# Soft mixture of experts behind attention: fp32 output product on four row groups, and where the expert weights are put

## The chip, the core and the metric

The kernel runs on one core of one Trainium2 chip. A core has TensorE (PE; its weight loads are shown apart as PEld), VectorE (DVE), ScalarE (ACT), GpSimd (POOL) and SyncE (SP); here SP issues all DMAs, in the order of its own program, and 16 DMA engines move the data. The metric is the device time of one execution in microseconds, the median of several runs.

## The reference

Causal attention with a decay bias, over 8 batches, 8 heads, 576 tokens and 64 features a head; its output, 4608 tokens by 512, goes through a soft mixture of 8 experts with 4 slots each.

```python
scores = q @ k.T / sqrt(64);  bias = min(-(cum[t] - cum[s]), 0)   # cum: running sum of max(s, 0)
attn = softmax(where(causal, scores + bias, -1e9));  x = attn @ v   # x: [4608, 512]
logits = x @ phi                                                    # [4608, 32]
d = softmax over tokens (logits);  slot_input = d.T @ x             # [32, 512], 4 slots an expert
h = max(slot_input[e] @ w1[e], 0);  slot_out[e] = h @ w2[e]         # w1 [512, 1024], w2 [1024, 512]
c = softmax over slots (logits);  out = c @ slot_out                # [4608, 512] in fp32
```

The expert weights are 32 MB, the output is 9.4 MB; all of it is fp32 in memory.

## The kernel before, in words

**Attention.** 64 heads are worked off as 32 pairs (p = 0 to 31), four pairs a batch. For each pair: load, cast into a high and a low part, row maxima, scores, exponentials, causal cuts, product with v, normalisation, and transposes back to rows of tokens. At the end of each batch the logits are formed (`lt`, L632 and L636) and the slot inputs are summed up (`t2` to `t8`). `e_nat` keeps the 32 exponentials of each token, divided by their sum (`s2p`, on POOL), as five chunks a batch: four of 128 tokens and one of 64.

**Order.** Every step is an entry of `ops` with an engine, a cost, a due time and what it comes after. `schedule` (L44) makes the order from these, for all engines; the steps of the last stretch are left out of it and follow in an order written out by hand in `END` (L33). Each engine works strictly in its own order. SP's loads and fetches are entries like the others.

**Weights.** Each expert matrix is cut into 4 quarters of 512 KB, [128, 1024] in SBUF; w1 and w2 together have 64. `seq` (L897) lists them in the order of use: all of w1, then w2 for the first half of the output columns, then w2 for the second. `pre` is a buffer for 21 quarters (`NPRE`) that are loaded during attention. 22 more (`room`, L883, steps `get`) go to places that attention is done with: three slots `g`, one slot `w` of two places, and 17 places of the `arena`, a buffer that holds attention's working tiles side by side. `ended` (L876) says after which steps a tile of the arena is dead. That makes 43; the other 21 are loaded (`refill`, L963) over w1 quarters that the first expert product has used.

**Experts.** `mlp1` (L970) multiplies the 32 slot inputs (`sit`) with w1 for four experts at a time, on four groups of 32 columns; `relu` and `turn` (L988) give the transposed hidden values. `mlp2` (L1000) does the second product for one half of the output columns and four experts, in 8 steps of 4 groups. `pick` (L1011) takes each slot's row of its own expert with two 0/1 matrices, `sel`, that are part of the constants loaded early (`cst_sb`).

**Output.** For each batch `sp` splits `e_nat` into a rounded part, a rest, and the rounded part again (3 x 32 columns), `ct` (L719) transposes the five chunks on TensorE, and `cd` copies them to SBUF: 96 rows of slots by tokens. These stand between the steps of the second product's first half (loop at L1070). `pick` leaves the picked rows in three parts too, split in the same way. The output product (L1038) is then one pass in fp32r with 96 rows, 128 tokens by 256 columns each; two go into one PSUM bank, VectorE and ScalarE copy the banks out in turn (L1040, L1042), and every 8 tiles or 512 KB a DMA writes 512 tokens' half rows (L1046). `result(0)` runs beside the second product's second half, `result(1)` after it.

Of the kernel before, what the change touches and what calls it, by code (L numbers as in the profile page):

```python
# [30 lines left out]
NPRE = 21  # L31

END = """  # L33
s.31.0 ev.29 load_v.31 z.30.3 s.31.3 rd.29 ex.31.0.0 s.31.1 ex.31.0.1 rd.28 cut.31.0 s.31.2 ex.31.1.1 ex.31.1.0
sm.30 ex.31.3.1 get.4 ex.31.3.0 a.30.0 ex.31.2.0 e1.7.1.0 cut.31.3 ex.31.2.1 a.30.1 zc.31 cut.31.2 cut.31.1
z.31.0 a.30.2 a.30.3 nr.29 a.30.4 rb.30 ev.30 get.8 z.31.1 get.9 get.7 a.31.0 z.31.2 z.31.3 ax.31 a.31.1 nr.28
evx.31 nr.30 sm.31 a.31.2 e1.7.2.0 get.14 a.31.3 a.31.4 rb.31 ev.31 get.13 get.12 t5.6 nr.31 lt.28 t6.6 lt.29
get.16 lt.30 get.10 lt.31 t7.6 get.15 c0.7 t2.7 nat0.7 t8.6 t3.7 nat.30 nat.28 natd.30 m.0 nat.29 natd0.7 t4.7
nat.31 m.1 natd.28 get.18 t5.7 natd.29 get.11 natd.31 m.2 get.17 t6.7 m.3 m.4 busy.3 t7.7 m.5 c1.7 t8.7 get.21
m.6 get.19 m.7 get.20 s0.7 busy.5 sit.0 s1.7 sit.1 s2.7 s2p.7 s2p.6  # L40
# [72 lines left out]
def tile_attn_softmoe(ctx: ExitStack, tc, qk, v, s, phi, w1, w2, cst, out):  # L113
# [17 lines left out]
    cst_sb = top.tile([128, 2 * 96 + 128], F32, name="cst_sb")  # L131
    sel = [cst_sb[:, 0:96], cst_sb[:, 96:192]]
    g4 = cst_sb[:, 192:320]
# [13 lines left out]
    sit = top.tile([128, DM // 128, NS], F32, name="sit")  # L147
# [6 lines left out]
    size = dict(raw=2 * S, p=3200, u=S, v=640, z=2 * S, r=S, x=NCH * DM)  # L154
    place = [(kind, (NP + i) % n) for kind, n in (("raw", NR), ("p", NPB), ("z", NZ), ("v", NV), ("r", NQ), ("u", NU), ("x", 1))
             for i in range(n)]
    ar, o = {}, 0
    for key in place:
        ar[key] = o
        o += size[key[0]]  # L160
    arena = top.tile([128, o], F32, name="arena")
# [36 lines left out]
    onesl = one.tile([128, 4 * HP, 32], F32, name="onesl")  # L198
    nc.vector.memset(onesl, 0.0)
    for a in range(4 * HP):  # L200
        nc.vector.memset(onesl[:, a, a:a + 1], 1.0)
# [8 lines left out]
    ph = one.tile([128, HP, 4 * NS], F32, name="ph")  # L210
# [10 lines left out]
    for i, t in enumerate(gs):  # L221
        if i == 1:

            mask = one.tile([128, S], F32, name="mask")
            nc.gpsimd.memset(mask, 0.0)
            nc.gpsimd.affine_select(mask[:, S - 128:S], mask[:, S - 128:S], pattern=[[-1, 128]], compare_op=ALU.is_ge,
                                    fill=NEG, base=0, channel_multiplier=1)
# [36 lines left out]
    def scores(p):  # L264
# [59 lines left out]
        def red(i, a):  # L324
# [125 lines left out]
    def pair(p):  # L450
# [55 lines left out]
        def sm():  # L506
# [93 lines left out]
    late_ct = []  # L600

    def batch(b):
# [21 lines left out]
        def lt(hp):  # L624
# [6 lines left out]
            for g in range(4):  # L631
                nc.tensor.matmul(st["lt", b][32 * g:32 * g + 32, 64:192], ph[:, hp, 32 * g:32 * g + 32],  # L632
                                 st["u", p][:, 64 + 128 * g:192 + 128 * g], start=hp == 0, stop=hp == HP - 1)

            for g in range(4):
                nc.tensor.matmul(st["lt", b][32 * g:32 * g + 32, 0:64], ph[:, hp, 32 * g:32 * g + 32],  # L636
# [22 lines left out]
        def c0():  # L659
            l = p2.tile([128, 192], F32, tag="ls", name=f"ls{b}", bufs=1)  # L660
# [45 lines left out]

        def sp(i):
            x = e_nat[:, b * NCH:(b + 1) * NCH, :]
            if i == 0:
                st["en", b] = p2.tile([128, NCH, 3, NS], F32R, tag="en", name=f"en{b}")  # L710
            en = st["en", b]
            if i == 0:
                nc.vector.tensor_copy(en[:, :, 0, :], x)
            elif i == 1:
                nc.scalar.copy(en[:, :, 2, :], x)
            else:
                nc.vector.tensor_tensor(en[:, :, 1, :], x, en[:, :, 0, :].bitcast(F32), op=ALU.subtract)

        def ct():  # L719
            en = st.pop(("en", b))  # L720
            st["ct", b] = pa, pb = bank(f"cta{b}"), bank(f"ctb{b}")
            for c in range(NCH):
                dst = pa[0:96, 128 * (c - 1):128 * c] if c else pb[0:96, 0:128]
                nc.tensor.transpose(dst, en[:, (c - 1) % NCH].rearrange("p l s -> p (l s)").bitcast(F32), ident)  # L724

        def cd():
            if "ctw" not in st:
                st["ctw"] = [slot("w", [96, min(4, B - 4 * i), S], F32R, f"ct{i}") for i in range((B + 3) // 4)]
            ct = st["ctw"][b // 4][:, b % 4]
            pa, pb = st.pop(("ct", b))  # L730
            copy = nc.vector.tensor_copy if b % 2 else nc.scalar.copy
            copy(ct[:, 64:576], pa[0:96, :])
            copy(ct[:, 0:64], pb[0:96, 0:64])
        late_ct.append((sp, ct, cd))
# [69 lines left out]
    def m1():  # L804
        mrow = one.tile([1, 4, NS], F32, name="mrow")
# [39 lines left out]
    def sit1():  # L845
        nc.vector.tensor_copy(sit, st.pop("sit")[:, 0:128].rearrange("p (c s) -> p c s", c=NCC))
# [23 lines left out]
    op(("cst",), "SP", 450, (3.0,), (fetch, cst_sb, cst), [("load", 3)], dma=450)  # L870
    op(("cw",), "SP", 450, (2.5,), lambda: nc.sync.dma_start(out=cumd, in_=cumhl), [("cum", 1)], dma=800)
    op(("phi",), "SP", 650, (2.0,), load_phi, [("load", 2)], dma=728)
# [3 lines left out]
    def ended(kind, i):  # L876
        n = dict(raw=NR, p=NPB, z=NZ, v=NV, r=NQ, u=NU, x=1)[kind]
# [3 lines left out]
                    x=[("t7", B - 1)])[kind]  # L881
# [7 lines left out]
    for i in range(o // F):  # L889
# [80 lines left out]
    def mlp1(eg):  # L970
        pss = [bank(f"m1{eg}{half}") for half in range(F // 512)]
        for cc in range(NCC):
            for half in range(F // 512):
                for g in range(4):
                    nc.tensor.matmul(pss[half][32 * g:32 * g + 32, :], sit[:, cc, :],
# [22 lines left out]
    sl = []  # L998
# [12 lines left out]
    def pick(half):  # L1011

        ps = bank(f"sel{half}")
        for eg in range(2):
            nc.tensor.matmul(ps[0:96, 0:HC], sel[eg], sos[half][:, eg, :], start=(eg == 0), stop=(eg == 1))  # L1015
        t = sl[half]
        nc.scalar.copy(t, ps[0:96, 0:HC])  # L1017
        nc.vector.tensor_tensor(t[64:96, :], ps[64:96, 0:HC], t[64:96, :].bitcast(F32), op=ALU.subtract)  # L1018

    NO = NT // 128  # L1020
# [5 lines left out]
    def result(half, beside=iter(()), pace=()):  # L1026
        k = 0
        outc = out[:, HC * half:HC * half + HC].rearrange("(t p) c -> p t c", p=128)
        for i in range(0, NO, 4):
            m = min(4, NO - i)  # L1030
            ot = stage.pop(0)[:, 0:m * HC].rearrange("p (t c) -> p t c", t=m)
            for j in range(0, m, 2):
                n = min(2, m - j)
                po = bank(f"po{half}_{i + j}")[:, 0:n * HC].rearrange("p (t c) -> p t c", t=n)
                for x in range(n):
                    b, c = divmod(i + j + x, 9)
                    cv = st["ctw"][b // 2].rearrange("p b s -> p (b s)")[:, 1152 * (b % 2) + 128 * c:1152 * (b % 2) + 128 * c + 128]
# [101 lines left out]
```

## Time and profile before

| | us |
|---|---|
| median of three runs | 437.86 (437.07 to 438.16) |
| the profiled execution: time, span | 438.36, 436.60 |
| TensorE busy in the span | 409.5 |
| VectorE, ScalarE, GpSimd busy | 308.5, 246.0, 281.2 |
| attention ends, first expert product starts | about 370.8 |
| first output DMA issued | 403.4 |
| last matmul | 422.2 |

Times in the profile count from the start of the span. The windows view gives for stretches of time each engine's busy time with its instruction count, then the TensorE clock that was granted (1.00 is full), the mean share of the DMA engines that is busy and the rate in GB/s. The timeline lists instructions in order of time with start and duration, alike ones merged and counted (x8). The chain of waits is followed back from the last instruction. A plain fp32 matmul shows as two instructions (two passes), an fp32r one or a transpose as one. A shape such as 128\*32 means 128 rows by 32 columns of the array.

### The profile page before, as it was taken

To read this page: it belongs to the slowest core of one execution; us is meant where nothing else is said; L and a number is where in the kernel's file an instruction comes from. 1 tells how busy PE (TensorE), PEld (TensorE's weight loads), DVE (VectorE), ACT (ScalarE), POOL (GpSimd) and SP (SyncE) were. 2 spreads that over 40 slices of the span, in tenths; PEclk is the share of its full clock that TensorE was granted. 3 is DMA by queue.
4 is the path that set the end of the run, shared out by engine and by line. 5 is a ranking of instruction groups with operands and counts; after the bars stand their busy time and mean duration, and the time that the engine had idled before them with its cause. 6 is when DMAs were issued, how large, how long until landed. Compare 5 with 4: busy or idle time off the path is not lost. (4 is left out here: it accounts for less than half of the span.)

```text
span 436.6 us, 14785 instructions
## 1 busy us (share of the span) xinstructions
PE 409.5 (94%) x5671; PEld 304.9 (70%) x5671; DVE 308.5 (71%) x1058; ACT 246.0 (56%) x730; POOL 281.2 (64%) x385
## 2 busy tenths in 40 slices
PE   8899999989999999999999999999999999999960
PEld 7687778777777777776777777678777867345550
DVE  6777766987887788779867887788778465045360
ACT  2246676576657665766576658567655744133360
POOL 7349889879877887788778878886888710000000
PEclk9699999999999999999999999999999999999995
DMA  5317556635674466446644742272238589999798
GB/s 176 109 58 233 164 162 170 199 101 173 197 195 127 142 196 180 131 138 193 181 134 136 207 120 86 89 191 89 84 99 227 191 259 371 409 408 388 264 325 289
DMA packets 54118, 82.90 MB, mean 190 GB/s; under 512 B 5280, under 2 KB 41376, under 8 KB 54048
## 3 DMA queue, kind: packets, MB, share of 16 engines
q1 hardware_dynamic: 54048, 81.95, 59.8%
q8 instruction: 45, 0.74, 0.7%
q14 instruction: 25, 0.20, 0.2%
HBM read 71.54 MB, written 10.03 MB: 187 GB/s over the span
## 5 line engine op out<-in xcount | busy, mean ns | idle before, releaser
L333 DVE CUSTOM_DVE_ANT_0 junk<-mx,mask 128x448 bf16<-128x448 f32 (+3 forms) x320 | 125.6, 427 | 52.0 <-POOL arena L405 24.7
L398 ACT ACTIVATE arena<-s 128x288 f32<-128x288 f32 (+4 forms) x384 | 114.3, 409 | 30.3 <-PE s L387 29.6
L387 PE MATMUL s<-w 64*128 64x288 f32 (+4 forms) x1152 | 109.4, 304 | 0.0
L488 PE MATMUL y<-arena 128*64 128x512 f32 (+4 forms) x640 | 90.2, 427 | 0.0
L387 PEld LDWEIGHTS s<-w 64*128 64x128 f32 (+1 forms) x1152 | 81.9, 177 | 10.0 <-issue 1.3
L405 POOL TENSOR_SCALAR_AFFINE_SELECT arena<-arena 128x256 f32<-128x256 f32 (+1 forms) x160 | 66.5, 428 | 23.7 <-ACT arena L398 21.6
L488 PEld LDWEIGHTS y<-arena 128*64 128x64 f32 x640 | 43.0, 137 | 45.6 <-issue 34.6
L431 POOL TENSOR_TENSOR arena<-arena 128x896 f32<-128x896 f32 x31 | 67.5, 2177 | 7.4 <-PE mt L356 5.3
L321 PE MATMUL mx<-w 64*128 64x288 f32 (+4 forms) x384 | 58.8, 311 | 4.5 <-DVE e_nat L677 2.7
L387 PE MATMUL s<-g 64*128 64x288 f32 (+4 forms) x384 | 56.7, 291 | 0.0
L321 PE MATMUL mx<-g,ones 64*128 64x288 f32 (+4 forms) x384 | 55.3, 305 | 0.7 <-POOL g L231 0.7
L433 POOL TENSOR_TENSOR arena<-arena 128x640 f32<-128x640 f32 x31 | 47.9, 1546 | 2.6
L288 ACT CAST w<-arena 128x576 fp32r<-128x576 f32 x64 | 39.8, 675 | 15.3 <-DMA arena<-in_qk_dram 15.3
L293 DVE TENSOR_TENSOR w<-arena,w 128x576 fp32r<-128x576 f32 x64 | 48.3, 780 | 0.0
L321 PEld LDWEIGHTS mx<-w 64*128 64x128 f32 x384 | 40.9, 188 | 8.6 <-PE s L387 3.8
L500 ACT COPY arena<-y 128x512 f32<-128x512 f32 x32 | 18.8, 588 | 45.2 <-PE y L488 45.2
L321 PEld LDWEIGHTS mx<-g,ones 64*128 64x128 f32 x384 | 40.6, 189 | 1.3 <-POOL g L231 0.9
L387 PEld LDWEIGHTS s<-g 64*128 64x128 f32 (+1 forms) x384 | 35.3, 176 | 0.6 <-DMA g<-hl 0.2
L550 DVE TENSOR_TENSOR arena<-arena 128x576 f32<-128x576 f32 x30 | 30.4, 1023 | 5.7 <-DMA arena<-rs 5.4
L348 POOL TENSOR_SCALAR mh<-mx 128x10 fp32r<-128x10 f32 x32 | 21.7, 677 | 18.7 <-DVE mx L333 18.7
L435 POOL TENSOR_TENSOR arena<-arena 128x384 f32<-128x384 f32 x31 | 31.5, 1015 | 2.4
L333 DVE CUSTOM_DVE_ANT_0 junk<-mx,mask,mx 128x288 bf16<-128x288 f32 x64 | 30.6, 515 | 2.4 <-PE mx L321 1.2
(161 smaller groups left out, 563.3 us busy)
## 6 DMA issues: line engine op xcount, KB each, us to landing
pre<-in_w_dram SPq DMA_DIRECT2D x41, 512.0 KB
arena<-in_qk_dram SPq DMA_DIRECT2D x32, 576.0 KB
arena<-in_w_dram SPq DMA_DIRECT2D x17, 512.0 KB
arena<-rs SPq DMA_DIRECT2D x60, 144.0 KB
arena<-in_v_dram SPq DMA_DIRECT2D x32, 256.0 KB
out_dram<-arena SPq DMA_DIRECT2D x13, 512.0 KB
out_dram<-pre SPq DMA_DIRECT2D x5, 512.0 KB
wg<-in_w_dram SPq DMA_DIRECT2D x3, 512.0 KB
```

Source lines behind the costliest of these rows:

```text
L288: nc.scalar.copy(w[:, QO + S * i:QO + S * (i + 1)], st["raw", p][:, i, :])
L293: nc.vector.tensor_tensor(w[:, QO + S * (2 + i):QO + S * (3 + i)], st["raw", p][:, i, :], w[:, QO + S * i:QO + S * (i + 1)].bitcast(F32), ...
L321: nc.tensor.matmul(ps[a][:, d:d + hi - lo], l[r], t[r, KO + lo:KO + hi], start=t is w, stop=t is gt)
L333: nc.vector.tensor_tensor_reduce(out=junk[r, 0:w], in0=ps[r, d:d + w], in1=mask[r, o:o + w], scale=1.0, scalar=m[:, a, 4:5] if i == 1 else ...
L387: nc.tensor.matmul(ps[a][0:n, d:d + hi - lo], t[r, ko + 128 * j:ko + 128 * j + n], t[r, qo + lo:qo + hi], start=x == 0, stop=x == 3)
L398: nc.scalar.activation(st["p", p][0:n, a, o + lo:o + hi], ps[0:n, d:d + hi - lo], AF.Exp, bias=0.0, scale=0.125)
L405: nc.gpsimd.affine_select(d, d, pattern=[[0, 2], [1, n]], compare_op=ALU.is_ge, fill=0.0, base=0, channel_multiplier=-1)
L431: eng.tensor_tensor(z[:, :, 128:576], pt[:, :, 128:576], pt[:, :, 576:1024], op=ALU.add)
L433: eng.tensor_tensor(z[:, :, 256:576], z[:, :, 256:576], pt[:, :, 1024:1344], op=ALU.add)
L435: eng.tensor_tensor(z[:, :, 384:576], z[:, :, 384:576], pt[:, :, 1344:1536], op=ALU.add)
L488: nc.tensor.matmul(y[r, lo - 64:512], vt[:, j, r], st["p", p][:, g, OFF[j] + lo - 128 * j:OFF[j] + 576 - 128 * j], start=(j == 0), stop=(j ...
L550: nc.vector.tensor_tensor(u, u, st.pop(("r", p)), op=ALU.mult)
```

## The change

- **Output product.** `sp`, `cd` and the old `ct` are gone. `ct(k)` transposes the four chunks of 128 tokens of four batches at a time, so that chunk g lies on rows 32g to 32g + 31, and copies them back over `e_nat`; the four chunks of 64 tokens go through four small products into `dn`. `pick` makes four copies of the picked rows, one for each group of 32 rows, in plain fp32. The product of chunk g then runs on row group g, into a PSUM bank of its own: `two` does half the columns of two batches, `whole` all 512 columns of one batch, `heads` the 64-token chunks of four batches with whole rows. Batches 0 to 5 go through `two`, 6 and 7 through `whole`.
- **Order at the end.** `ct(0)` stands ahead of the first expert product, `ct(1)` within it. Beside the second product's second half go `two(0)`, `two(2)`, `two(4)` for the first half of the columns; after it `whole(6)`, `whole(7)`, both `heads`, then `two` for the second half.
- **Weights.** 50 instead of 43 quarters have places of their own: 23 in `pre`, and 27 in `room` (all three `w` slots and an 18th place of the arena, which now holds `mask`, `phi` and `ls` too). 14 are refilled.
- **Constants.** `sel` (now 128 columns each) is no longer loaded early: SP fetches it after the last refill into a w1 quarter that has been used. `phi` is loaded once instead of four times side by side, `onesl` is one row of zeros with a column of ones that is read at different offsets, `mask` is 448 columns wide.
- `END` is written anew. `s2p.6` stands near its start instead of its end, `load_v.31` and `rd.29` have changed places on SP.

The core of the diff:

```diff
-NPRE = 21
+NPRE = 23
-    size = dict(raw=2 * S, p=3200, u=S, v=640, z=2 * S, r=S, x=NCH * DM)
+    size = dict(raw=2 * S, p=3200, u=S, v=640, z=2 * S, r=S, x=NCH * DM, mask=S - 128, phi=HP * NS, ls=192)
...
-        for i in range(1 if kind == "w" else n):
+        for i in range(n):
             for x in range(2 if kind == "w" else 1):
                 room.append(((kind, i, x), [("s", NP - n + i, y) for y in range(4)]))
...
+    def ct(k):
+        pa, pb = bank(f"ct{k}"), bank(f"cs{k}")
+        for i in range(4):
+            nc.tensor.transpose(pa[:, 128 * i:128 * i + 128], et[:, 4 * k + i, 0:128], ident)
+        for i, r in enumerate(rows):
+            nc.tensor.matmul(pb[r, 0:64], et[0:64, 4 * k + i, 128:160], ident[0:64, 0:64], start=True, stop=True)
+        (nc.scalar.copy if k else nc.vector.tensor_copy)(et[:, 4 * k:4 * k + 4, 0:128], pa.rearrange("p (b t) -> p b t", b=4))
+        nc.scalar.copy(dn[:, k, 0:64], pb[:, 0:64])
...
-            nc.tensor.matmul(ps[0:96, 0:HC], sel[eg], sos[half][:, eg, :], start=(eg == 0), stop=(eg == 1))
-        t = sl[half]
-        nc.scalar.copy(t, ps[0:96, 0:HC])
-        nc.vector.tensor_tensor(t[64:96, :], ps[64:96, 0:HC], t[64:96, :].bitcast(F32), op=ALU.subtract)
+            nc.tensor.matmul(ps[:, 0:HC], sel[eg], sos[half][:, eg, :], start=(eg == 0), stop=(eg == 1))
+        nc.scalar.copy(so[:, HC * half:HC * half + HC], ps[:, 0:HC])
...
+    def two(b, half):
+        c = slice(HC * half, HC * half + HC)
+        po = [x.rearrange("p (b c) -> p b c", b=2) for x in banks(4)]
+        for i in range(2):
+            for x, r in zip(po, rows):
+                nc.tensor.matmul(x[:, i, :], et[r, b + i, 0:128], so[r, c], start=True, stop=True)
+        for j in (0, 2):
+            ot = stage.pop(0).rearrange("p (b j c) -> p b j c", b=2, j=2)
+            for x in range(2):
+                evict(ot[:, :, x, :], po[j + x])
+            for i in range(2):
+                nc.sync.dma_start(out=outb[b + i, 64 + 128 * j:320 + 128 * j, c].rearrange("(j p) c -> p j c", p=128),
+                                  in_=ot[:, i])
+    def whole(b):
+        po = banks(4)
+        for x, r in zip(po, rows):
+            nc.tensor.matmul(x, et[r, b, 0:128], so[r, :], start=True, stop=True)
...
+            nc.sync.dma_start(out=outb[b, 64 + 128 * j:320 + 128 * j].rearrange("(j p) c -> p j c", p=128), in_=ot)
...
-    busy(2)
+    so = again[late + 1][:, 0:DM]
+    sel = [again[late + 1][:, DM + 128 * eg:DM + 128 * eg + 128] for eg in range(2)]
+    ct(0)
     m = mlp1(0)
...
         refill(16 + 4 * cc, 20 + 4 * cc)
+        if cc == 0:
+            ct(1)
         if cc == 1:
+            fetch(again[late + 1][:, DM:DM + 256], cst[:, 128:384])
             turn(0)
...
-    for b in range(B):
-        steps(m, 2)
-        if b == 3:
-            turn(1)
-        late_ct[b][1]()
-        split(b + 2)
-        late_ct[b][2]()
+    steps(m, 5)
+    turn(1)
     steps(m)
...
+    m = chain(mlp2(1, 0), mlp2(1, 1))
+    steps(m, 1)
     pick(0)
...
-    result(0, rest(), (2, 3, 3, 3, 3, 3, 1))
-    result(1)
+    steps(m, 1)
+    NA = 6
+    for b in range(0, NA, 2):
+        two(b, 0)
+        steps(m, 4)
+    steps(m)
+    pick(1)
+    late_banks = True
+    for b in range(NA, B):
+        whole(b)
+    for k in range(2):
+        heads(k)
+    for b in range(0, NA, 2):
+        two(b, 1)
```

More of the change, by code (lines that the diff above doesn't have):

```diff
@@ L197, in tile_attn_softmoe @@
     SQ = S // 8
-    onesl = one.tile([128, 4 * HP, 32], F32, name="onesl")
+    onesl = one.tile([128, 4 * HP + 31], F32, name="onesl")
     nc.vector.memset(onesl, 0.0)
-    for a in range(4 * HP):
-        nc.vector.memset(onesl[:, a, a:a + 1], 1.0)
+    nc.vector.memset(onesl[:, 4 * HP - 1:4 * HP], 1.0)
     dn = one.tile([128, 2, 128], F32, name="dn")
@@ L209, in tile_attn_softmoe @@
         nc.gpsimd.memset(reg("p", i).rearrange("p (a x) -> p a x", a=2)[64:128, :, 1536:1600], 0.0)
-    ph = one.tile([128, HP, 4 * NS], F32, name="ph")
+    ph = reg("phi", 0).rearrange("p (h s) -> p h s", h=HP)
     QO, KO = PAD, PAD + S
@@ L704, in batch @@
         op(("s2p", b), "POOL", 415, (T + 0.2, "soft", *late), s2p, [("s2", b)])
[L707 to L734, printed above, removed]
         def t2():
@@ L804, in m1 @@
     def m1():
-        mrow = one.tile([1, 4, NS], F32, name="mrow")
+        mrow = p2.tile([1, 4, NS], F32, tag="hl", name="mrow")
         st["mrow"] = mrow
@@ L974, in mlp1 @@
                 for g in range(4):
-                    nc.tensor.matmul(pss[half][32 * g:32 * g + 32, :], sit[:, cc, :],
+                    nc.tensor.matmul(pss[half][32 * g:32 * g + 32, :], st["in"][:, cc, :],
                                      w1q[4 * eg + g, cc][:, 512 * half:512 * half + 512],
@@ L997, in tile_attn_softmoe @@
     HC = DM // 2
-    sl = []
+    rows = [slice(32 * g, 32 * g + 32) for g in range(4)]
+    et = e_nat.rearrange("p (b c) s -> p b (c s)", b=B)
+    def ct(k):
[6 more added lines that the diff above has]
+        nc.scalar.copy(dn[:, k, 0:64], pb[:, 0:64])
     def mlp2(half, eg):
@@ L1024, in steps @@
             next(it, None)
[L1026 to L1037, printed above, removed]
-                    nc.tensor.matmul(po[:, x, :], cv, sl[half], start=True, stop=True)
-                if k % 2 == 0:
-                    nc.vector.tensor_copy(ot[:, j:j + n, :], po)
-                else:
-                    nc.scalar.copy(ot[:, j:j + n, :], po)
-                k += 1
-            if i // 4 < len(pace):
-                steps(beside, pace[i // 4])
-            nc.sync.dma_start(out=outc[:, i:i + m, :], in_=ot)
@@ L1048, in tile_attn_softmoe, with evict, banks @@
-    busy(2)
+    outb = out.rearrange("(b t) c -> b t c", b=B)
+    turns = [0, 0]
+    def evict(dst, src):
+        turns[0] += 1
+        (nc.scalar.copy if turns[0] % 2 else nc.vector.tensor_copy)(dst, src)
+    def banks(n):
+        turns[1] += 1
+        if turns[1] % 2 == 0 and late_banks:
+            return [bank("po") for _ in range(n - 2)] + [psy.tile([128, 512], F32, tag=t, name="po") for t in ("y", "sum")]
+        return [bank("po") for _ in range(n)]
+    def two(b, half):
[11 more added lines that the diff above has]
+                                  in_=ot[:, i])
@@ new lines, in whole, with heads @@
+    def whole(b):
+        po = banks(4)
+        for x, r in zip(po, rows):
+            nc.tensor.matmul(x, et[r, b, 0:128], so[r, :], start=True, stop=True)
+        for j in (0, 2):
+            ot = stage.pop(0).rearrange("p (j c) -> p j c", j=2)
+            for x in range(2):
+                evict(ot[:, x, :], po[j + x])
+            nc.sync.dma_start(out=outb[b, 64 + 128 * j:320 + 128 * j].rearrange("(j p) c -> p j c", p=128), in_=ot)
+    def heads(k):
+        po = banks(2)
+        for i, r in enumerate(rows):
+            nc.tensor.matmul(po[i // 2][64 * (i % 2):64 * (i % 2) + 64, :], dn[r, k, 0:64], so[r, :], start=True, stop=True)
+        ot = stage.pop(0).rearrange("p (j c) -> p j c", j=2)
+        for x in range(2):
+            evict(ot[:, x, :], po[x])
+        for i in range(4):
+            nc.sync.dma_start(out=outb[4 * k + i, 0:64], in_=ot[64 * (i % 2):64 * (i % 2) + 64, i // 2, :])
```

76 lines of the change are left out of this document (32 added, 44 removed).

## Prediction

> **What bounds the kernel now.** I read the page first, for the stage in which something other than TensorE is full.
>
> ```profile
> DMA  5317556635674466446644742272238589999798
> ...
> pre<-in_w_dram SPq DMA_DIRECT2D x41, 512.0 KB
> ...
> out_dram<-arena SPq DMA_DIRECT2D x13, 512.0 KB
> out_dram<-pre SPq DMA_DIRECT2D x5, 512.0 KB
> ```
>
> For thirty slices the DMA engines have room; in the last nine they are full but for a dip. Weights and outputs both go in pieces of 512 KB: 64 of weights (32 MB), 18 of output. The windows over that stage come next (columns: stretch, length, PE, PEld, DVE, ACT and POOL busy, clock, DMA share, GB/s).
>
> ```profile
> 370.00:380.00 10.00, 10.00 (x95) 3.52 (x98) 0.88 (x4) 1.32 (x3) 0.87 (x2) 1.00 1.03 410
> ...
> 390.00:400.00 10.00, 10.00 (x126) 5.96 (x119) 6.26 (x18) 3.52 (x11) 0.00 (x0) 1.00 1.03 409
> ...
> 420.00:430.00 10.00, 2.23 (x14) 1.60 (x12) 2.94 (x5) 2.36 (x5) 0.00 (x0) 0.68 1.03 339
> ```
> ```profile
> 344.00:346.00 2.00, 2.00 (x19) 0.89 (x19) 1.93 (x5) 1.22 (x5) 1.92 (x2) 1.00 0.07 22
> ...
> 352.00:354.00 2.00, 2.00 (x21) 1.04 (x18) 1.49 (x3) 0.59 (x2) 0.65 (x2) 1.00 0.83 217
> ...
> 402.00:404.00 2.00, 1.96 (x22) 1.24 (x23) 0.69 (x1) 0.59 (x1) 0.00 (x0) 1.00 0.68 270
> ...
> 408.00:410.00 2.00, 2.00 (x28) 1.12 (x28) 1.02 (x2) 0.59 (x1) 0.00 (x0) 1.00 0.80 273
> ...
> 422.00:424.00 2.00, 0.23 (x2) 0.02 (x1) 0.94 (x2) 0.74 (x2) 0.00 (x0) 0.92 1.02 339
> ...
> 434.00:436.00 2.00, 0.00 (x0) 0.00 (x0) 0.00 (x0) 0.00 (x0) 0.00 (x0) 0.50 0.47 157
> ```
>
> A full share is 1.03. Weights (rows of 4 KB) then flow at 409 GB/s, 1.28 us for a quarter of 524,288 bytes; outputs (rows of 1 KB) at about 341, 1.54 us for as much, 3.07 us for a megabyte of two such pieces. Around 408 outputs flow at only 273. The last byte leaves at 434 + 2 x 0.47 / 1.03 = 434.9, 1.7 before the span's end at 436.6. What SP issued when:
>
> ```profile
> 354.18 14.70 SPq L852 DMA_DIRECT2D arena<-in_w_dram  x15
> 372.69 12.19 SPq L852 DMA_DIRECT2D pre<-in_w_dram  x12
> 385.84 0.33 SPq L852 DMA_DIRECT2D ww<-in_w_dram  x1
> 387.12 9.22 SPq L852 DMA_DIRECT2D pre<-in_w_dram  x8
> 403.43 12.11 SPq L1046 DMA_DIRECT2D out_dram<-arena  x7
> ```
>
> From 354.2 on 36 quarters are issued, 46.1 us of flow. They begin at about 355.5, lose about 1.6 to a lower share up to 364, and end at 355.5 + 46.1 + 1.6 = 403.2, which the 402 to 404 row bears out. SP's last refill (396.3) is some 7 us ahead of the flow: it stands in line. So the closing stage is weights until 403, then outputs, the first of them held up by TensorE. The chain of waits and the PE timeline show why:
>
> ```profile
> 390.28 0.24 PE ctb L724
> 390.53 0.44 PE cta L724 x4
> 390.96 1.00 PE m L1006 x16
> ...
> 400.26 0.88 PE sel L1015 x4
> ...
> 401.16 0.38 ACT sl L1017
> ...
> 401.56 0.43 DVE sl L1018
> ...
> 408.65 1.43 PE m L1006 x24
> 410.08 0.67 PE po L1038 x4
> ```
> ```profile
> 370.76 5.36 PE L975 MATMUL m<-pre,sit 128*32 128x512 f32 x48
> ...
> 385.67 1.05 PE L1006 MATMUL m<-arena,ww 128*32 128x256 f32 x16
> ...
> 391.89 1.09 PE L992 MATMUL ht<-ident,wg 128*128 128x128 f32 x8
> ```
>
> TensorE goes without a break from 370.76: first expert product to 385.67, second product in 0.43 us a step (two steps and a switch of tile mode, 1.00), with eight sets of five transposes (0.24 + 0.44 = 0.68 each) between. The first output waits for 400.26 + 0.88 + 0.38 + 0.43. Then one 512 KB piece per 2.10 us (1.43 + 0.67), or 250 GB/s.
>
> **The weights.** Two more quarters go into the early buffer, in stages where DMA has room: nothing, covered. Four more get slots that the scores of pairs 30 and 31 release, and one more arena place appears. Pair 30's scores end near 340.6, pair 31's near 350.7:
>
> ```profile
> 340.29 0.31 PE L387 MATMUL s<-g 64*128 64x320 f32 x2
> ...
> 350.28 0.45 PE L387 MATMUL s<-g 64*128 64x448 f32 x2
> ```
>
> In the written closing order one of the new slots comes before the list begins, two stand ahead of SP's first wait on the last products, the fourth stands nearly last. So five quarters (two early, three in slots) are through before 355.5, in the rows with shares of 0.07 to 0.83; 31 remain instead of 36. The weights end at 403.2 - 5 x 1.28 = 396.8. The other new places only change which copy is overwritten later. SP's new order also moves the loads of pair 29's reciprocals ahead of the last value load; both land several us before their readers, and what that could delay on TensorE is covered by the wait below. Setup loses sixteen 1-column fills and two smaller loads, all beside other work: 0.
>
> **TensorE up to the first output.** Removed: eight sets of transposes, 8 x 0.68 = 5.4 us, with their casts and copies on ACT and VectorE. Added: two sets of four transposes and four 64-row products, by the rows above 0.44 + 0.2 each; the first replaces filler, the second moves the first product's end to 386.6 with its mode switches. Then 16 steps x 0.43 + 1.09 for L992 + a switch: the second product's first half ends at 394.7, its next step at 395.2. The split of the picked rows on VectorE (0.43) goes.
>
> Now a wait is added. The picking matrices (128 KB) no longer arrive at the start; SP fetches them after its last refill, so they stand behind every weight in the one queue. They flow at 396.8 + 0.35. With 0.3 for the slowest of the 16 engines and about 1.0 until the semaphore (estimate; between 0 and the 1.7 that lay behind the last byte), TensorE can pick at 398.5. It has been idle since 395.2: **3.3 us**, and all that is queued behind the pick on TensorE waits, the second product's second half too. Pick 0.88, copy 0.38 and hops: the first output product starts at 399.8.
>
> **What an idle TensorE costs.** The clock rows:
>
> ```profile
> 14.44 0.42 PE L321 MATMUL mx<-w 64*128 64x64 f32 x2 [1.76 <-POOL w L233]
> ```
> ```profile
> 13.50:14.00 0.50, 0.00 (x0) 0.00 (x0) 0.50 (x5) 0.00 (x0) 0.50 (x2) 1.00 0.00 0
> 14.00:14.50 0.50, 0.06 (x2) 0.06 (x2) 0.50 (x3) 0.00 (x0) 0.44 (x4) 0.58 0.04 9
> ...
> 20.50:21.00 0.50, 0.50 (x8) 0.50 (x6) 0.00 (x0) 0.00 (x0) 0.00 (x0) 0.59 0.04 16
> ...
> 423.50:424.00 0.50, 0.00 (x0) 0.00 (x0) 0.00 (x0) 0.00 (x0) 0.00 (x0) 0.68 1.05 354
> ```
>
> After 1.76 us of waiting the clock fell to half at 14.08 and came back at 20.9, 6.8 us later; after the last matmul (422.2) it fell at 423.7, 1.5 us later; the 0.9 us gap at 401 cost nothing. So a 3.3 us wait halves the clock, for 3.4 us (half of the 6.8) to 6.8 us of work: a loss of 1.7 to 3.4 us. I take 2.4. The Trainium skill ("TensorE: Matmul & The Clock Gate", Part 1: The HAM clock gate) halves the clock after at least one idle window of about 3.4 us. By that, this wait would just escape and the sum below would lose its 2.4; the trace, with a fall after 1.5, differs, and I go by the trace.
>
> **The output product.** Before: 72 one-pass matmuls of 256 columns, 0.168 each (0.67 for four). After: two passes, four groups of 32 rows at once. A pass of 256 columns takes 0.215 (four in 0.86, the pick), so four tiles take 0.43 if groups overlap and 1.72 if not. Nearest row for rows:
>
> ```profile
> 338.19 0.80 PE L387 MATMUL s<-w 64*128 64x448 f32 x6
> 338.82 0.37 PE L387 MATMUL s<-g 64*128 64x448 f32 x2
> ```
>
> Six take 0.63, so two halves of 64 rows pass together at 0.21 a pair for 448 columns; four groups of 32 columns do so in the second product. I take 0.43. The Trainium skill (same page, Part 3: Packing small matmuls — row/col tiling) gives 3.07 instead of 4 for four such tiles; by that each megabyte would cost 0.26 more, under 0.8 us in all. Copies out:
>
> ```profile
> L1040 DVE COPY arena<-po 128x512 f32<-128x512 f32 x13 | 8.6, 686 | 7.9 <-PE po L1038 7.9
> L1042 ACT COPY arena<-po 128x512 f32<-128x512 f32 x13 | 7.5, 586 | 9.2 <-PE po L1038 8.7
> ```
>
> Two on each engine per megabyte, 1.4 us: under the 3.07 of its DMA. 36 issues at about 0.4 on SP are 14 us, also covered.
>
> **The sum.** From the first product's start T: 0.86, a copy 0.7, issue to flow 0.9 (an estimate: issued at 403.43, and the 402 row has room only for weights until 403.3), so outputs flow from T + 2.5. A megabyte per 0.86 + 4 steps + 0.14 = 2.72 us keeps up with 3.07, so three take until T + 11.7. TensorE meanwhile needs 3 x 2.72 + 2 x 0.43 + 1.7 (wait, pick, copy) = 10.7, then 0.9 + 0.8 + 0.9 to the next flow: T + 13.3, a 1.6 us gap. Left: 3.15 MB in rows of 2 KB and three half-row megabytes. Between 341 and 409 GB/s I take 386 for 2 KB (a fixed cost per row through both points; ends 7.7 and 9.2 us): 8.15 + 9.2 = 17.35. T + 30.65, and 1.7 to the span's end: T + 32.35 = 432.15. The slow clock adds its 2.4 to the chain ahead of the gap: 434.55. The profiled execution took 438.36 for a span of 436.60, 1.76 around it, and is 0.50 above the median of 437.86. So 434.55 + 1.76 - 0.50 = **435.8**.
>
> **The rivals.** *The wait leaves the clock alone.* For it: the gap of 0.9 that didn't touch it, and how near 3.3 is to one half of 6.8 if the clock should want a whole such stretch idle. Against: both falls after 1.5 to 1.8. Time 432.15 + 1.26 = 433.4. That is also what the Trainium skill's rule above would give.
>
> *The picking matrices arrive in time*, if SP's fetch isn't last in line or the rows before it land earlier. For it: the place they go to is free long before. Against: SP's 7 us lead over the flow. Then T = 395.1 + 1.3 = 396.4, span 428.75, time 430.0.
>
> *The row groups don't overlap* (the slower side). No row shows 32-row groups; against it stand the 64-row halves. Each megabyte costs 3.44 instead of 0.86 on TensorE, which replaces DMA as the bound as soon as it passes about 2.4 us. Next flow 3 x 2.58 later, then seven units of 3.44 and the last piece: T + 47, about 448.
>
> *The new slots bring nothing early*: their loads queue behind others, only the two early quarters count, weights end at 400.6. TensorE idles 7 us; T = 403.6, with the slow clock 439.6.
>
> **How the numbers follow.** Forecast 0.50, warm clock 0.18, matrices in time 0.17, groups apart 0.07, slots useless 0.08. A measurement of this kernel tells about 0.3%, 1.3 us, from no change: 436.5 to 439.2 is the same. Of the forecast (433.5 to 438.5 by its bounds: clock loss, 2 KB rate, landing) 0.33 is faster, 0.15 same, 0.02 slower; the two fast rivals add 0.35, the groups 0.07 slower, the slots 0.04 and 0.04. Faster 0.68, same 0.19, slower 0.13. The range 429.5 to 438.8 leaves out the groups, half of the slots and what is below the second rival.
>
> **What would show it.** Last weight issue near 390; first output issue near 401.5 (398 if the matrices are in time); TensorE idle some 3 us ahead of the pick with a DMA as releaser; clock below 1.00 between 397 and 407; four output tiles in 0.43; DMA at 1.02 from about 413 to 432 with 341 and 386 GB/s. A first output before 399, a flat clock, or output products above 2.4 us a megabyte would prove me wrong.

## The result, and the profile after

The changed kernel takes 441.38 us, median of 20 runs (437.4 to 444.16), beside 437.9 for the kernel before (20 runs, 436.16 to 438.65): ratio 1.0072, 95% interval 1.0051 to 1.0094. It is slower by 0.7%, where 435.8 was forecast, and lies above the predicted range of 429.5 to 438.8. Ratios and intervals, here and below, leave disturbed runs out; medians are of all runs.

The profiled execution of the changed kernel took 438.52 us for a span of 436.7, almost as the one before (438.36 and 436.60). That is chance, and the first thing to be read off, in the PE timeline of after:

```profile
367.78 5.36 PE L943 MATMUL m<-pre,sit 128*32 128x512 f32 x48
...
397.61 2.08 PE L994 MATMUL sel<-pre 128*128 128x256 f32 x4 [5.26 <-DMA pre<-in_cst_dram]
400.63 1.79 PE L1020 MATMUL po<-pre,e_nat 32*128 32x256 f32 x16
404.21 1.15 PE L1020 MATMUL po<-pre,e_nat 32*128 32x256 f32 x16
...
412.68 2.00 PE L1033 MATMUL po<-pre,e_nat 32*128 32x512 f32 x16 [0.46 <-ACT pre L995]
414.96 2.19 PE L1044 MATMUL po<-pre,dn 32*64 32x512 f32 x16 [0.28 <-ACT pre L1006]
```

The first expert product starts at 367.78, in before at 370.76: attention happened to end 3.0 us sooner. Over the profiled executions with the changed kernel's attention, this one and those below, this start lies between 367.5 and 373.2, on average 370.8; the two with before's attention have 370.8 and 369.1 (e3). No change of attention itself shows. What can be compared from profile to profile is the **closing stretch**, from the first expert product to the end of the span: 436.60 - 370.76 = 65.8 us before, 436.7 - 367.78 = 68.9 after. That is 3.1 us more, close to the 3.5 of the medians. In the rest of the text "+24.6" means 24.6 us after the first expert product.

On the page of after, the DMA row is full in slices 33 to 36 and dips to 2 in the 37th, where before's last nine had no such hole, and 36 loads instead of 41 go into `pre`:

```profile
DMA  5317555626754476448534752461358599992898
...
pre<-in_w_dram SPq DMA_DIRECT2D x36, 512.0 KB
```

In the PE rows: TensorE stood for 5.26 us ahead of the first pick until a DMA of the constants landed, and the four picks then took 2.08 us, where the same four take 1.13 at the full clock (e1, below). The first output product took 1.79, the second 1.15. SP's timeline of after says where those constants stood in the queue:

```profile
370.31 14.61 SPq L819 DMA_DIRECT2D pre<-in_w_dram  x12
385.86 0.33 SPq L819 DMA_DIRECT2D arena<-in_w_dram  x1
387.13 0.33 SPq L819 DMA_DIRECT2D pre<-in_w_dram  x1
388.41 0.33 SPq L819 DMA_DIRECT2D pre<-in_cst_dram  x1
...
403.24 8.47 SPq L1026 DMA_DIRECT2D out_dram<-pre  x12
```

The last weight load is issued at 387.13 (+19.4), the picking matrices right behind it at 388.41, and they land 9.15 us later, as the chain of waits of after has it (start, length, what ran):

```profile
388.41 9.15 DMA pre<-in_cst_dram
```

A matrix of 128 KB, a third of a microsecond of flow, takes that long, which fits a queue in which all that was issued before it goes first: the weights flow until about 396 in the rows that follow. The windows of after show the rest of the stretch (columns as before: PE, PEld, DVE, ACT, POOL busy, clock, DMA share, GB/s):

```profile
392.00:394.00 2.00, 0.35 (x8) 0.00 (x0) 0.00 (x0) 0.36 (x1) 0.00 (x0) 1.00 1.00 399
394.00:396.00 2.00, 0.00 (x0) 0.00 (x0) 0.00 (x0) 0.00 (x0) 0.00 (x0) 0.79 0.90 354
396.00:398.00 2.00, 0.39 (x1) 0.39 (x2) 0.00 (x0) 0.00 (x0) 0.00 (x0) 0.50 0.14 54
...
400.00:402.00 2.00, 2.00 (x20) 1.22 (x16) 0.00 (x0) 0.10 (x1) 0.00 (x0) 0.50 0.00 0
402.00:404.00 2.00, 2.00 (x40) 0.94 (x32) 1.29 (x2) 1.07 (x2) 0.00 (x0) 1.00 0.00 0
404.00:406.00 2.00, 2.00 (x40) 1.18 (x36) 0.58 (x1) 0.63 (x2) 0.00 (x0) 1.00 0.93 305
...
414.00:416.00 2.00, 1.72 (x18) 0.79 (x14) 2.00 (x4) 1.89 (x4) 0.00 (x0) 1.00 0.24 94
416.00:418.00 2.00, 2.00 (x28) 1.04 (x24) 1.73 (x3) 1.17 (x2) 0.00 (x0) 1.00 1.04 374
...
422.00:424.00 2.00, 0.00 (x0) 0.00 (x0) 0.00 (x0) 0.00 (x0) 0.00 (x0) 0.62 0.84 219
424.00:426.00 2.00, 0.00 (x0) 0.00 (x0) 0.00 (x0) 0.00 (x0) 0.00 (x0) 0.50 0.90 205
426.00:428.00 2.00, 0.00 (x0) 0.00 (x0) 0.00 (x0) 0.00 (x0) 0.00 (x0) 0.50 0.99 342
...
434.00:436.00 2.00, 0.00 (x0) 0.00 (x0) 0.00 (x0) 0.00 (x0) 0.00 (x0) 0.50 0.57 203
```

Three places are to be seen. From 392.35 to 397.6 TensorE is idle, and from about 395.2 to 402.0 its clock is halved. From 398 to 404 the DMA engines move nothing at all: before had weights in flight until 403.2 and outputs right behind them. And between 422 and 426, when nothing computes any more, the flow is at 205 to 219 GB/s with a share of 0.84 to 0.90, where the rows shown above and below have 374 and 342: these are the eight pieces of `heads`, 64 partitions each.

### The profile page after: what moved, and what is told of

It reads as the page before. It is cut to its first block, busy times and chain, and to the rows that moved or that the text cites. A ratio compares the mean times of both kernels' runs of the same rounds, so it can differ in the third digit from the quotient of the medians.

```text
span 436.7 us, 14782 instructions
## 1 busy us (share of the span) xinstructions
PE 404.0 (93%) x5705; PEld 299.1 (68%) x5705; DVE 297.5 (68%) x1018; ACT 241.1 (55%) x717; POOL 281.7 (65%) x385
## 4 chain that ended last, share of the span: by engine, by line
PE 76%; DVE 7%; DMA 7%; issue 2%; POOL 2%; SPq 1%; ACT 1%; DVEq 0%
PE s L384 22%; PE y L485 17%; PE mx L318 12%; DMA arena<-rs 3%; PE sum L514 3%; PE m L943 3%; PE m L985 3%; DVE nmin L707 2%; PE nat L555 2%; PE busy L900 2%; DMA pre<-in_cst_dram 2%; PE lt L627 2%; PE sl L745 1%; PE po L1020 1%; PE mt L353 1%
## 5 line engine op out<-in xcount | busy, mean ns | idle before, releaser
L330 DVE CUSTOM_DVE_ANT_0 junk<-mx,arena 128x448 bf16<-128x448 f32 (+3 forms) x320 | 125.6, 427 | 54.1 <-POOL arena L402 25.6
L330 DVE CUSTOM_DVE_ANT_0 junk<-mx,arena,mx 128x288 bf16<-128x288 f32 x64 | 30.6, 516 | 2.2 <-PE mx L318 1.2
L330 DVE DVE_READ_ACCUMULATOR2_ANT mx<- 128x1 f32 (+1 forms) x384 | 31.6, 82 | 0.0
L547 DVE TENSOR_TENSOR arena<-arena 128x576 f32<-128x576 f32 x30 | 27.4, 924 | 5.8 <-DMA arena<-rs 5.6
```

Source lines behind the costliest of these rows:

```text
L330: nc.vector.tensor_tensor_reduce(out=junk[r, 0:w], in0=ps[r, d:d + w], in1=mask[r, o:o + w], scale=1.0, scalar=m[:, a, 4:5] if i == 1 else ...
L547: nc.vector.tensor_tensor(u, u, st.pop(("r", p)), op=ALU.mult)
```

## The experiments

Eleven kernels, each beside the kernel before on the same chip. The last column is the closing stretch of the profiled execution (65.8 before, 68.9 after).

| kernel | median us (range) | ratio to before, 95% interval | closing us |
|---|---|---|---|
| e1: matrices early | 434.43 (433.5 to 437.59) | 0.9909 (0.9876 to 0.9943) | 61.6 |
| e2: after with 44 fillers | 443.44 (442.04 to 446.31) | 1.0106 (1.0074 to 1.0138) | 71.4 |
| e3: before, matrices late | 447.12 (446.78 to 448.14) | 1.0189 (1.0159 to 1.0218) | 75.4 |
| e4: e1, two quarters fewer | 435.06 (433.39 to 438.02) | 0.9925 (0.9887 to 0.9962) | 61.3 |
| e2b: after with 22 fillers | 439.88 (436.43 to 558.38) | 1.0022 (0.9994 to 1.0049) | 67.2 |
| e5: e1, heads on two queues | 434.4 (432.3 to 435.35) | 0.9903 (0.9881 to 0.9926) | 61.8 |
| e6: e1, no whole rows | 434.32 (432.16 to 434.8) | 0.9895 (0.9871 to 0.9919) | 61.1 |
| e7: e5 and e6 | 432.0 (430.14 to 433.73) | 0.9854 (0.9829 to 0.9879) | 59.7 |
| e8: e1, seven quarters fewer | 439.04 (437.67 to 444.2) | 1.0029 (0.9998 to 1.006) | 65.8 |
| e9: e5 by GpSimd's queue | 435.19 (433.61 to 436.77) | 0.9924 (0.9893 to 0.9954) | 61.7 |
| e10: e7 by GpSimd's queue | 433.15 (429.4 to 434.39) | 0.986 (0.9819 to 0.99) | 59.8 |

**The matrices' place.** The theory was that the late fetch costs a wait and a halved clock and so outweighs what the change gains elsewhere; the rival, that the loss lies in the output product or the stores. e1 fetches the matrices ahead of all refills (SP issues them at 375.42, +2.2), into `acc`, which is dead by then:

```diff
-    sel = [again[late + 1][:, DM + 128 * eg:DM + 128 * eg + 128] for eg in range(2)]
+    sel = [acc[:, 128 * eg:128 * eg + 128] for eg in range(2)]
+    fetch(acc[:, 0:256], cst[:, 128:384])
...
-            fetch(again[late + 1][:, DM:DM + 256], cst[:, 128:384])
```

> The changed kernel, except that SP fetches the picking matrices into the summed slot inputs' tile as soon as that tile is dead (after the slot inputs are formed, near 367 us), ahead of all refills. Theory (the wait for the matrices and the halved clock behind it take the gain): TensorE picks at about 392.4 instead of 397.6, the clock stays 1.00, the first output is issued near 395.5, the DMA engines go from weights (until 396) to outputs without a break, 2 us of gap ahead of the whole rows: 395.9 + 9.2 + 2 + 5.5 + 4.9 + 9.2 + 1.6 = 428.3 of span, time about 430, ratio 0.982. Rival (the output path itself is slower: more and smaller DMAs, 64-row pieces, row groups): the wait only covered it, the time stays above 436, ratio 0.996 or more.

Measured: 434.43, ratio 0.9909. The PE timeline of e1:

```profile
373.24 5.36 PE L943 MATMUL m<-pre,sit 128*32 128x512 f32 x48
...
397.74 1.13 PE L994 MATMUL sel<-pre,acc 128*128 128x256 f32 x4
399.37 1.15 PE L1020 MATMUL po<-pre,e_nat 32*128 32x256 f32 x16
```

The pick follows with no wait at +24.5, just where after's TensorE fell idle (392.35, +24.6). The closing stretch is 7.3 us shorter than after's. One line decides the sign: the same change, with this fetch elsewhere, is 0.9% faster than before. The 430 of the theory was not reached, though; what is missing is worked out in the section on the prediction.

e3 is the other half of the proof: the kernel before, with only its picking matrices moved behind the last refill.

```diff
-    op(("cst",), "SP", 450, (3.0,), (fetch, cst_sb, cst), [("load", 3)], dma=450)
+    op(("cst",), "SP", 450, (3.0,), (fetch, cst_sb[:, 192:320], cst[:, 192:320]), [("load", 3)], dma=450)
...
+            fetch(cst_sb[:, 0:192], cst[:, 0:192])
```

> The kernel before, with one thing of the change: its picking matrices are fetched after the last refill instead of early, into the place they had. Theory: they land near 405, TensorE waits about 5 us ahead of the first pick, its clock halves for 3.4 us or more, and since its output stage is held up by TensorE all of it shows: 5 to 8 us more, 443 to 446, ratio 1.012 to 1.018. Rival (the late matrices are harmless and the loss lies in the output path): under 440, ratio below 1.005.

Measured: 447.12, ratio 1.0189, some 8 us and a little more than the 5 to 8 expected. Its PE timeline has the same wait and the same slow pick:

```profile
404.34 1.99 PE L1015 MATMUL sel<-pre,cst_sb 128*96 128x256 f32 x4 [5.69 <-DMA cst_sb<-in_cst_dram]
```

**Wait and clock apart.** Filler products ahead of the pick keep TensorE busy during the wait, into a PSUM bank that nothing reads:

```diff
+    d = bank("warm")
+    for i in range(44):
+        nc.tensor.matmul(d[:, 0:128], ident, ident, start=True, stop=True)
```

> The changed kernel with 44 filler products on TensorE ahead of the first pick (about 4.8 us of work), so that it waits as long but isn't idle. Theory (wait and clock are two costs): the pick still starts near 397.6, but takes 0.88 instead of 2.08, the clock stays 1.00, the first output is issued near 401.3 instead of 403.2; the time is about 2.2 us less than the changed kernel's in the same rounds, some 436 in a profile like the one of after, ratio 0.995 to 1.002, and the runs lie closer together than the 6.8 us of the changed kernel. Rival (the clock costs nothing, only the wait counts): no difference from the changed kernel, ratio 1.007.

Measured: 443.44, above after. The PE timeline of e2 shows why this run tells little:

```profile
397.56 10.09 PE L1080 MATMUL warm<-ident 128*128 128x128 f32 x88
407.49 1.03 PE L994 MATMUL sel<-pre 128*128 128x256 f32 x4
```

An fp32 product is two passes: 88 at 0.115 us ran on until 407.5, when the matrices, fetched at 395.28, must have landed about 404.4 (with after's 9.15 us). It only shows that the clock stays up: 1.03 us for the picks. The mended one has `range(22)`:

> After with 22 filler products (fp32, 128x128 by 128) in front of the picking products: 44 passes at the 0.115 us that a pass took in the run with 44 fillers, 5.06 us, so they end about when the picking matrices land (after's wait was 5.26 us). Theory (the wait and the halved clock are two costs that add): the picks still start at the matrices' landing, so the wait's cost stays, but sel's four picks take 0.9 to 1.1 us rather than 2.08 and the first output products run at the full clock; 2 to 3.5 us less than after, ratio to before 0.999 to 1.003, from slot inputs to the end 66 to 67.5 us where after has 69.7. Rival (the clock costs nothing because the chain goes by DMAs and PSUM reads): no difference to after, ratio about 1.007. The fillers' products go to a PSUM bank that nothing reads.

Measured: ratio 1.0022 (after 1.0072), closing 67.2 (after 68.9). The PE timeline of e2b:

```profile
395.36 5.18 PE L1080 MATMUL warm<-ident 128*128 128x128 f32 x44
401.42 1.13 PE L994 MATMUL sel<-pre 128*128 128x256 f32 x4 [0.88 <-DMA pre<-in_cst_dram]
...
403.05 1.15 PE L1020 MATMUL po<-pre,e_nat 32*128 32x256 f32 x16
```

Here the fillers end in time, and the pick still waits for the landing. From the pick's start to the first store on SP it is 3.6 us (401.42 to 405.00), as in e1 (397.74 to 401.33); in after it is 5.6 (397.61 to 403.24). So the halved clock cost 2.0 us, and the two costs add: 5.3 for the wait and 2.0 for the clock make the 7.3 between after and e1 (by the closing stretches of e2b and after the clock's part is 1.7). The rival without a price for the clock falls.

**The weights' places.** e4 is e1 with `NPRE = 21` instead of 23, e8 with `NPRE = 16`, which leaves 43 quarters with places of their own, as many as in before.

> As the first of these kernels, with 21 instead of 23 quarters in the early buffer, so that two more are refilled (48 places of their own). Theory (once the wait is gone the weights' flow sets the start of the outputs): the last weight lands 2.6 us later, near 398.5, and the time is 1 to 2.6 us above that of the first kernel. Rival (the places for weights don't matter, TensorE sets the end): within 0.7 us of the first kernel. The planner sees two loads fewer, so attention may come out up to some us different; the trace says by how much.

Measured: 435.06, closing 61.3 beside e1's 61.6. Two quarters fewer cost nothing that shows; the 1 to 2.6 us of the theory did not come.

> The matrices-early version (434.4 us) with the weights' places cut by seven quarters, so that 43 and not 50 can come early, as in before. Theory (the new places are worth what they take off the closing stream of transfers): seven quarters of 1.28 us, 8.9 us, come back into the stream; its free time there (about 0.9 us at 400 to 402 us, 1.7 us at 412 to 414 and some 0.5 us in between) takes up 3 us of it, so the end is 5 to 6 us later, 439 to 441 us, ratio to before 1.003 to 1.007. Rival (TensorE's products and the stores behind them set the end, as the run with two quarters fewer suggests, which cost nothing): within 1.5 us of 434.4, ratio 0.988 to 0.995.

Measured: ratio 1.0029 (e1 0.9909), closing 65.8: 4.3 us more than e1, so the theory holds, a little below its size. The PE timeline of e8 shows what e1's does not have, waits for weights within the second product:

```profile
407.33 0.62 PE L985 MATMUL m<-pre,arena 128*32 128x256 f32 x2 [0.22 <-DMA pre<-in_w_dram]
408.59 1.91 PE L985 MATMUL m<-pre,arena 128*32 128x256 f32 x26 [0.64 <-DMA pre<-in_w_dram]
```

So the first two of seven quarters are covered and the others are worth 4.3 us. e8, with fp32 row groups, whole rows, no late fetch and as many places as before, has before's closing stretch to 0.1 us. That does not make the new output product worth nothing, because e8's weights come later than before's. The DMA queue view gives packets, MB and share from the first expert product on, for before and, below, e8:

```profile
q1 hardware_dynamic: 13183, 22.80, 93.3%
```
```profile
q1 hardware_dynamic: 12432, 24.22, 98.5%
```

Without the 9.44 MB of output, and in e8 without the 0.13 MB of the matrices, 13.36 MB of weights were left in before and 14.65 in e8: 2.5 quarters more, 3.2 us of flow at 409 GB/s. e8 has five places fewer in the early buffer than before and five more in places that attention has to release first. So the rest of the change makes up for about as much as these quarters cost; no run separates the two.

**Stores.** e5 issues the odd pieces of the heads from ScalarE, so that a piece of the upper 64 partitions can go beside one of the lower:

```diff
-            nc.sync.dma_start(out=outb[4 * k + i, 0:64], ...)
+            (nc.scalar if i % 2 else nc.sync).dma_start(out=outb[4 * k + i, 0:64], ...)
```

> The matrices-early version (434.4 us), with the odd pieces of the eight heads (64 partitions of 2 KB rows) issued from ScalarE's queue and the even ones from SyncE's. Theory (a piece of 64 partitions reaches only half of the DMA engines' ways at a time, so that two pieces from different halves of the partitions, in flight together, move at the rate of a whole one): the heads' 1.05 MB take about 2.8 us at 374 GB/s rather than some 4.9 at 205 to 226, and the end comes 1.5 to 2.2 us earlier, ratio to before 0.986 to 0.988. Rival (the rate belongs to the piece, whatever its queue, or to a row of 2 KB in 64 partitions): the DMA rate between the whole batches and the last half rows stays at 205 to 226 GB/s, and the time at 434.4.

Measured: 434.4, no gain. The windows of e5 over the heads, and then ScalarE's timeline:

```profile
414.00:416.00 2.00, 0.82 (x12) 0.49 (x10) 1.26 (x2) 0.59 (x1) 0.00 (x0) 1.00 1.03 309
416.00:418.00 2.00, 0.64 (x8) 0.21 (x4) 1.29 (x2) 0.00 (x0) 0.00 (x0) 1.00 0.99 328
418.00:420.00 2.00, 0.11 (x2) 0.11 (x3) 0.00 (x0) 0.75 (x2) 0.00 (x0) 1.00 0.73 228
```
```profile
415.48 3.67 ACTq L1049 DMA_DIRECT2D out_dram<-ww  x2
419.25 0.59 ACT L1006 COPY wg<-po 128x512 f32<-128x512 f32 x1 [3.80 <-DMA out_dram<-ww]
```

The rows over 300 GB/s are not the heads' own rate. By the queues of e5 from 410.3 to 418 (q1 is SP's, q10 ScalarE's), SP's had moved no more by 418 than the 2.10 MB of the whole rows that stand ahead of its heads:

```profile
q1 hardware_dynamic: 1082, 2.09, 75.9%
q10 hardware_dynamic: 123, 0.21, 12.8%
```

Heads of both halves can have been in flight together only after that, and there the rate is 228 GB/s (418 to 420, where the flow runs thin at a share of 0.73) and 250 (420 to 422, half rows included). ScalarE stood for 3.67 us in issuing its second pair of pieces, and the copies of the last half rows behind them came late. So the time is the rival's, and the theory's rate is hardly tested.

e6 is e1 with `NA = 8`: all batches in half rows, no `whole`.

> The matrices-early version with all eight batches in half rows (no whole rows). Theory (whole rows of two batches cost more in the stall that they open, share 0.20 between 412 and 414 us, and in the slow heads than they gain by their longer rows): the stores run through at 341 to 350 GB/s, the 2 us gap closes and the heads' slow 4.9 us become 3.1, longer rows' gain of some 0.6 is lost: 2 to 3 us less than the matrices-early version, 431.5 to 432.5 us. Rival (the gap is only moved, since the later input of the second weights' half is what it waits for): within 0.7 us of 434.4, or above it.

Measured: 434.32, closing 0.5 us shorter. The gap is gone (no window between 402 and 412 is below 0.86), but the heads are no faster (167 and 203 GB/s from 414 to 418, below); they run on one queue all the same; my theory's 2 to 3 us did not come, and its claim that the heads would speed up was wrong. e7 has both edits.

> The matrices-early version with no whole rows and with the odd pieces of heads, if any are left, on ScalarE's queue. Theory (the two edits' gains lie on one path and add as far as heads are left): not above the better of the two single edits, about 431 to 432 us. Rival (each closes the same gap, or issuing from ScalarE delays its evictions): like the run with no whole rows alone, or 0.5 to 1 us above it.

Measured: 432.0, ratio 0.9854, closing 59.7. Here the sides of 64 do go side by side (from 414 to 416 SP's queue moves 0.26 MB and ScalarE's 0.21) and ScalarE waits less, 1.84 us at most. The windows of e6 and, below, of e7 over the heads:

```profile
412.00:414.00 2.00, 2.00 (x38) 1.80 (x35) 1.52 (x3) 1.46 (x3) 0.00 (x0) 1.00 0.94 270
414.00:416.00 2.00, 2.00 (x27) 1.75 (x29) 2.00 (x4) 1.92 (x5) 0.00 (x0) 1.00 0.72 167
416.00:418.00 2.00, 0.84 (x10) 0.39 (x6) 2.00 (x4) 1.41 (x3) 0.00 (x0) 1.00 0.89 203
```
```profile
412.00:414.00 2.00, 1.60 (x24) 1.11 (x20) 1.48 (x4) 0.29 (x1) 0.00 (x0) 1.00 0.95 286
414.00:416.00 2.00, 1.13 (x12) 0.70 (x12) 1.37 (x3) 0.55 (x2) 0.00 (x0) 1.00 0.78 233
416.00:418.00 2.00, 1.62 (x24) 1.23 (x28) 0.77 (x2) 2.00 (x5) 0.00 (x0) 1.00 0.94 296
```

In these 6 us e6 moves 2 x (270 + 167 + 203) = 1280 KB, e7 2 x (286 + 233 + 296) = 1630: 350 KB more, 1.0 us of flow at 341, and the closing stretch is 1.4 us shorter. How much of this is the heads' rate stays open: in the one row that is nearly all heads of both halves (414 to 416) e7 has 233 GB/s at a share of 0.78, only 6 to 14% above 205 to 219, and its half rows are issued sooner (416.36 against 417.42). e7 is the fastest kernel of this study, 1.5% below before.

Last, ScalarE's issues were given to GpSimd, which has nothing to do there (`nc.gpsimd` for `nc.scalar`).

> The version with the heads' pieces on two queues, the odd ones on GpSimd's queue rather than ScalarE's. Theory (two 64-partition pieces side by side do move faster, 309 to 328 GB/s in the ScalarE version, but its evictions of the last half rows waited 3.8 us behind its own issues, so that the flow ran dry at 418 to 420 us): GpSimd has no evictions to hold up, the rate stays above 300 GB/s and no gap follows, 1.3 to 2.2 us less than the ScalarE version, 432.2 to 433 us. Rival (GpSimd's issues are slow or late, or the gap comes from the stores' room): at 434.4 or above.

> No whole rows and the odd heads' pieces on GpSimd's queue. Theory (the same; in the ScalarE version the evictions waited 1.84 and 1.45 us behind issues and the share fell to 0.78 at 414 to 416): 0.3 to 1 us less than the ScalarE version's 432.0, 431 to 431.7 us. Rival: at 432.0 or above.

Measured: 435.19 and 433.15, closing 61.7 and 59.8, both as by ScalarE (61.8 and 59.7). In both the rival came true. No dry spell follows the heads in e9, but GpSimd issued its four pieces by 415.3 (412.94 + 2.31), while SP's four, behind the whole rows in its queue, were issued from 413.76 to 420.2: GpSimd's queue moved its 0.52 MB from 416 to 420, SP's heads came mostly after that, and the windows from 418 to 422 show 239 to 244 GB/s. The theory that ScalarE's waits were what ate the gain does not hold as a sum. In e7 and e10 both sides are issued at the same time, in e5 and e9 they are not, and only the first two gain; but they also lack the whole rows, so that the reason is not shown.

## Why the prediction was wrong

The mechanism that it put its chance on is what happened: the picks wait for the matrices at the end of the one queue, and the wait halves the clock. The sizes were off, all but one to the same side, so that the sign turned. Two steps failed above all: the number of weight quarters that are through early, and the rate of the heads. From the first expert product, the forecast was a closing stretch of 434.55 - 370.76 = 63.8 us. Measured: 68.9. The 5.1 us between are these terms.

- **Matrices' landing, 2.1 us: the first step that failed.** "So five quarters ... are through before 355.5", worth 6.4 us. TensorE's part was right (idle predicted from +24.4, measured +24.6), and so was SP's: its last weight load was predicted near 390, which is +19.2, and came at +19.4. But the pick, predicted at 398.5 (+27.7), started at +29.8, and the wait was 5.26 and not 3.3. What was left from the first expert product on is in the DMA queue view; before's row stands at e8 above, after's is:

```profile
q1 hardware_dynamic: 11516, 20.89, 82.8%
```

  Without output and matrices 13.36 MB of weights were left in before and 11.32 in after. That is 2.04 MB or 3.9 quarters fewer, not five: 5.0 us at 409 GB/s, not 6.4. At the prediction's 355.5, 15.3 us ahead of the first expert product, the same view says 2.8 quarters (28.27 and 26.93 MB in all, the latter with the matrices): the two early ones and about one of the three in slots. The quarters were all issued as early as I counted, 31 being left from 351.06 on (-16.7). What I missed is that the three in slots (four loads from -25.3 to -18.5, where before had one) come just ahead of that stream of 31; from there on a load takes off the stream's end only the idle share that it fills, and before's mean share in the last 20 us was already 0.93 of a full 1.03. The windows of these 20 us, before and, below, after:

```profile
350.76:370.76 20.00, 20.00 (x328) 14.43 (x328) 12.95 (x33) 7.62 (x24) 1.05 (x3) 1.00 0.93 326
```
```profile
347.78:367.78 20.00, 19.40 (x324) 14.02 (x312) 13.13 (x34) 7.11 (x24) 1.77 (x5) 1.00 0.97 357
```

  The rival in which the new slots bring nothing early was thus partly right. The other 0.7 us lie at the stream's end: the 11.45 MB with the matrices take 28.0 us at 409 GB/s, and the pick came 1.8 us behind that where 1.3 was allowed; before's own stream is 0.2 us longer by the same reckoning than I had it.

- **The heads, 2.2 us.** "3.15 MB in rows of 2 KB ... I take 386." The whole rows did flow at 374 GB/s, but a third of those bytes, 1.05 MB, are the heads, which I had put down by their row length alone. At about 210 GB/s they take 5.0 us instead of the 2.8 at 374. The Trainium skill ("SBUF — State Buffer", Door 1: The DMA port swizzle) gives 196 GB/s for 64 partitions against 328 for 128, at 1 MiB, since such a range reaches half of the ports; the trace agrees, with 205 to 219 against 374. The same page of the Trainium skill ("Can I just issue two DMAs to hit both halves?") says that two transfers to the two halves serialize and gained only 6%. The runs here do not decide that: e7's row with heads of both halves has 233 GB/s, 6 to 14% above the heads alone, and its 27% more bytes than e6 in 6 us include other stores.

- **Hops and the gap, 1.2 us.** From the pick to the first output product at full clock 1.6 us (e1: 397.74 to 399.37), predicted 1.3. From that product to the restart of the flow after the gap I had 13.3; in after the flow restarts at about 415.5, as the 414 to 416 row's 188 KB take 0.5 us at 374, which is 14.9, 0.65 of it the slow clock. A megabyte's cycle of products is 2.94 (404.21 to 407.15 in after), not 2.72. The gap was predicted at 1.6 and is 1.9 (the shares 0.24 and 0.86 from 412 to 416).

- **The clock, 0.4 us the other way.** 2.4 was taken within 1.7 to 3.4, and 2.0 was measured. It was at half for the 6.8 us that the first such case of before's trace had shown, but 2.4 of these were idle. The warm-clock rival is refuted by 2.08 us for the picks. The fall came near 395.2, 2.8 us after the last matmul's end; the Trainium skill's rule ("TensorE: Matmul & The Clock Gate", Part 1: The HAM clock gate) has a half clock after at least one idle window of about 3.4 us; the trace differs, with a fall after 2.8 us here as after 1.5 in before.

Right as predicted: the row groups overlap (eight tiles of two passes in 1.15 us, the row at 404.21, where 0.86 was forecast and 3.44 would be the sum one after another), so the slower-side rival never came up; the freed transposes (TensorE was ready at +24.6); the tail of 1.6 us. The rival in which the matrices arrive in time said 430.0, and e1, which makes it true, takes 434.4: by the closing stretch 58.0 (428.75 - 370.76) against 61.6, of which the heads and the hops make 3.4.

What nets out against before, by closing stretches: the late matrices cost 7.3 us (after against e1), and all the rest of the change together brings 4.3 (e1 against before), so after is 3.1 longer. In the rest are the quarters, of which e1 has 4.6 fewer left than before at the first expert product (10.94 MB, 20.51 in all by the same view, against 13.36), and the new output product; e8 shows that the seven places alone are worth 4.3, but at the first expert product it has fewer weights loaded than before, so the two are not told apart. Not tried either: what the fp32 groups bring without whole rows and without any new place.

## What to carry to other kernels

A small load that something waits for costs the whole length of the queue it is put behind, so place it ahead of the long stream in its queue, not where its room becomes free; here one line moved the result from 0.7% slower to 0.9% faster. Count an earlier load only as far as it fills idle share of the DMA engines: of five quarters issued early, 3.9 showed as through at the first expert product. And cost a store by the partitions it reaches as well as by its row length.

## What the hardware showed that I had not expected

- Stores of 64 partitions with 2 KB rows: 205 to 219 GB/s alone, where 128 partitions had 374 with 2 KB rows and about 341 with 1 KB rows. The DMA share stays at 0.84 to 0.90 meanwhile, so the share doesn't show that half of the rate is missing.
- An engine that issues a DMA can stand in the issue: two pieces on ScalarE took 3.67 us, and the copies behind them waited.
- Attention's end moved between 367.5 and 373.2 us from one profiled execution to the next, with the same steps in it. Two profiles are to be compared from a common event on, not from the start of the span.
